# One attention-and-MLP kernel, the same instructions in a newly searched order

## The chip, the cores and the metric

The kernel runs on 1 core of one Trainium2 chip. The metric is the device time of an execution in microseconds (us); lower is better. A core has five engines that run side by side: PE multiplies matrices (PEld is its weight load), DVE and ACT do elementwise work, POOL (GpSimd) does some of that too, and SP issues most of the transfers.

## The reference

Attention over 4 batches, 8 heads, 768 positions and head size 64, in which a position sees itself, the 127 positions before it and the first 4 positions (the "sinks"); then one gated MLP block on the result, with a matrix over the positions.

```python
keep = is_sink | in_window                      # 4 sinks, window 128
a = softmax(where(keep, q @ k.T / 8, -1e9))
x = (a @ v)  as (batch, 768, 512)
h = gelu_tanh(x @ w_in)                         # 512 -> 1024
u, v = h[..., :512], h[..., 512:]
v_n = (v - mean) / sqrt(var + 1e-6) * g_ln
v_s = einsum('ts,bsd->btd', w_sg, v_n) + b_sg   # over the 768 positions
out = x + (u * v_s) @ w_out
```

## The kernel before

The heads are taken two at a time: pair n (0 to 15) holds two heads of batch b = n // 4. All work is cut into 854 named steps. Each step belongs to one engine and is made by a small function; the steps' data dependencies become semaphore waits. What this case is about is the order of the steps. It is written out in two tables: `FIRST` lists all 854 names, and `TAKERS` names the engine for steps that two engines can do. `Planner.run` goes through `FIRST` and emits one step after the other. Every engine then works through its own steps strictly in that order, so a step that waits holds up all later steps of the same engine, and SP's transfers are queued the same way. Buffers are handed out in this order too: a step that needs a buffer waits for the last reader of the tile that had it. There are 4 PSUM banks of the kind called `m` (most matmul results), 2 double banks of the kind called `s` (scores), and 4 buffers each for loaded k, q and v rows and for output rows.

The names, by stage:

- Attention, pair n: `load_k`, `load_q`, `load_v` (SP transfers), `cast_k`, `cast_q`, `cast_v` (to bf16), `turn_k`, `turn_q` (PE transposes into PSUM), `cols_k`, `cols_q` (copies out of PSUM); for pairs 11 to 15 a transposing transfer `dma_k`, `dma_q` on SP takes the place of turn and cols. `sc{n}{g}` are the score matmuls of block group g = 0, 1, 2, `exp{n}{g}` the exponentials on ACT, `band{n}{g}` the masking behind them. For the first four pairs there is no band step: `dark{n}{g}` puts the mask into PSUM ahead of the scores. `pv{n}{c}` multiplies by the values for half c of the positions, and `rcp{n}{c}` and `x{n}{c}` (both DVE) divide by the sums. `turn_x`, `cols_x`, or the transfer `xT`, transpose x.
- Sinks: `raw_a`, `raw_b` load the sinks' values, `low_a` and `low_b` convert them, `vsink_a1` to `vsink_b3` copy them on SP, `zero_*` clear their place. `low_b` stands for 12 pairs, `low_a` for 4. `load_k4` and all later loads stand behind `vsink_b3` on SP.
- MLP, batch b: `hv{b}{j}` and `gelu_v`, `bn` (statistics, DVE), `rstd{b}0` and `rstd{b}3` (POOL, three position tiles each), `shift`, and `vn{b}{j}` (normalised v, DVE or ACT); `hu{b}{f}{m}` and `gelu_u`; `sp{b}{f}{m}a` and `b` (the two halves of the product with w_sg), `gate` and `gT` (DVE); `pj{b}{t}` (product with w_out), `o` (DVE, adds x) and `store`.
- `w_in_v`, `w_in_u`, `wsg0`, `wsg1`, `w_out` load weights on POOL's queue; `turn_w` and `cols_w` transpose w_sg.

The PE order alternates between batches: the attention of batch b + 1 lies between the spatial products of batch b. `exp` and the gelus need different ACT tables, so the gelus of a batch wait until the exponentials of one pair are done.

Of the kernel before, what the change touches and what calls it, by code (L numbers as in the profile page):

```python
# [49 lines left out]
class Planner:  # L50
# [37 lines left out]


FIRST = (  # L90
    "load_k0 iden load_q0 raw_a night blank nil zero_a3 zero_a1 zero_b3 warm zero_a0 dark mask "
# [64 lines left out]
    "peek_DVE copied look"  # L156
)
TAKERS = (
    "zero_a0:ACT zero_a1:DVE zero_a2:DVE zero_a3:DVE low_a:DVE zero_b0:DVE zero_b1:DVE "
    "zero_b2:ACT zero_b3:DVE low_b:POOL cols_g:DVE cols_w0:DVE cols_w1:ACT cols_w2:ACT "  # L160
    "cols_w3:DVE cols_w4:DVE cols_w5:DVE cast_k0:POOL cols_k0:DVE cast_q0:POOL cols_q0:ACT "
    "cols_x0:ACT cast_k1:POOL cols_k1:DVE cast_q1:POOL cols_q1:DVE cols_x1:ACT cast_k2:POOL "
    "cols_k2:DVE cast_q2:DVE cols_q2:DVE cols_x2:DVE cast_k3:POOL cols_k3:ACT cast_q3:POOL "
    "cols_q3:DVE cols_x3:DVE vn00:DVE vn01:DVE vn02:ACT vn03:ACT vn04:DVE vn05:DVE cols_k4:DVE "
    "cols_q4:ACT band41:POOL band42:POOL cols_k5:ACT cols_q5:ACT band51:POOL band52:POOL "
    "cols_k6:ACT cols_q6:ACT band61:POOL band62:POOL cols_k7:ACT cols_q7:ACT band71:POOL "
    "band72:DVE cols_x7:DVE cols_k8:ACT cols_q8:ACT band81:DVE band82:POOL vn10:DVE vn11:DVE "
    "vn12:DVE vn13:DVE vn14:DVE vn15:DVE cols_k9:ACT cols_q9:ACT band91:POOL band92:POOL "
    "cols_k10:ACT cols_q10:ACT band101:POOL band102:POOL band111:POOL band112:POOL cols_x11:ACT "
    "band121:POOL band122:POOL vn20:DVE vn21:DVE vn22:ACT vn23:ACT vn24:ACT vn25:DVE "  # L170
    "band131:POOL band132:POOL band141:POOL band142:POOL band151:POOL band152:POOL cols_x15:ACT "
    "vn30:DVE vn31:ACT vn32:ACT vn33:ACT vn34:DVE vn35:DVE"
)
# [1168 lines left out]
```

## Time and profile before

| what | before |
|---|---|
| time, median of 3 runs | 161.76 us (161.67 to 161.82) |
| the profiled execution's own time | 163.07 us |
| its span, first to last instruction | 161.1 us |
| granted TensorE clock | 0.996 |
| PE busy | 150.1 us, 93% of the span |
| DVE busy | 130.5 us, 81% |
| ACT busy | 107.5 us, 67% |
| POOL busy | 83.6 us, 52% |
| transfers | 32.42 MB, mean 201 GB/s |

The profiled execution took 1.31 us more than the median of the runs. The engines' busy times overlap, so they don't add up to the span. A row of the profile's time line reads: start in us, us taken, engine, line of the kernel, operation, what it writes and reads, how many instructions are merged in it, and in square brackets how long the engine had been idle and what ended that. A row of the table of stretches reads: from and to in us, length, then busy us and number of instructions of PE, PEld, DVE, ACT and POOL, the clock, the share of the transfer engines and GB/s.

### The profile page before, as it was taken

Reading aid. Unit: us, or ns where it says so; the run is one execution under the profiler, and the core shown is the slowest. Engines: PE = TensorE matmul, PEld = TensorE weight load, DVE = VectorE, ACT = ScalarE, POOL = GpSimd, SP = SyncE. Lnnn points to the kernel's source line nnn. Section 1 sums busy time; section 2 is a strip of 40 time slices with the busy share of each in tenths; the row PEclk is TensorE's granted clock in tenths of the full one; section 3 lists DMA queues with packets and bytes.
Section 4 is the critical chain, followed back from the end, with each engine's and each line's share of the span. In section 5 each row is a group of like instructions: output and inputs, shape, how many; then the busy total and the mean of one; then the engine's idle time right before and its main releaser. Section 6 shows DMA issues by size and latency. Waiting matters only on the chain. (4 is left out here: it accounts for less than half of the span.)

```text
span 161.1 us, 4001 instructions
## 1 busy us (share of the span) xinstructions
PE 150.1 (93%) x1547; PEld 87.3 (54%) x1562; DVE 130.5 (81%) x283; ACT 107.5 (67%) x143; POOL 83.6 (52%) x126
## 2 busy tenths in 40 slices
PE   6789999998899999999989999999999999999980
PEld 2335665566656766546556555555556645555540
DVE  7555678695898989969999979868999969888980
ACT  6168878695989877988857778665997168811100
POOL 3465761228688789067975880865579602300000
PEclk9999999999999999999999999999999999999998
DMA  4999999998999986999988889999993340140163
GB/s 146 299 270 305 205 151 206 168 289 231 358 336 240 342 130 163 241 315 234 215 142 209 209 177 216 206 300 257 241 216 114 90 158 0 50 148 4 65 259 141
DMA packets 67877, 32.42 MB, mean 201 GB/s; under 512 B 56564, under 2 KB 64772, under 8 KB 67856
## 3 DMA queue, kind: packets, MB, share of 16 engines
q1 hardware_dynamic: 65328, 29.26, 69.5%
q0 software_dynamic: 2384, 2.75, 10.8%
q8 instruction: 13, 0.21, 0.6%
q10 hardware_dynamic: 144, 0.13, 0.2%
q14 instruction: 8, 0.07, 0.1%
HBM read 24.81 MB, written 6.29 MB: 193 GB/s over the span
## 5 line engine op out<-in xcount | busy, mean ns | idle before, releaser
L627 ACT ACTIVATE ex<-sc 128x1024 bf16<-128x1024 f32 x48 | 47.4, 1024 | 10.5 <-PE sc L610 10.4
L864 PE MATMUL vs<-wsgT,vn 128*128 128x384 bf16 x192 | 35.5, 326 | 1.6 <-DVE vn L840 1.0
L864 PEld LDWEIGHTS <-vn 128*128 128x128 bf16 x192 | 17.5, 98 | 13.2 <-issue 1.6
L793 PE MATMUL hu<-xT,w_in_sb 128*128 128x384 bf16 x128 | 23.4, 326 | 0.0
L801 ACT ACTIVATE uT<-hu 128x384 bf16<-128x384 f32 x32 | 14.9, 490 | 12.3 <-PE hu L793 12.1
L907 PE MATMUL o_ps<-w_out_sb,gT 128*128 128x512 bf16 (+1 forms) x91 | 22.6, 370 | 0.5
L751 PE MATMUL hv<-w_in_sb,xT 128*128 128x512 bf16 x94 | 22.4, 379 | 0.1
L875 DVE SCALAR_TENSOR_TENSOR vs<-vs,g_sb,b_bc 128x384 f32<-128x384 f32 x32 | 19.5, 619 | 2.6 <-PE vs L864 1.3
L773 DVE BATCH_NORM_STATS2 st<-v_all 128x6 f32<-128x512 f32 x24 | 16.3, 678 | 6.5 <-ACT v_all L762 6.5
L311 POOL TENSOR_SCALAR_AFFINE_SELECT ex<-ex 128x512 bf16<-128x512 bf16 (+1 forms) x23 | 15.4, 670 | 9.7 <-ACT ex L627 9.4
L610 PE MATMUL sc<-qT,kT 64*128 64x256 bf16 (+2 forms) x320 | 18.9, 249 | 0.9 <-ACT qT L247 0.5
L249 POOL CAST cast<-k_f 128x768 bf16<-128x768 f32 x16 | 13.4, 840 | 12.0 <-DMA k_f<-in_k_dram 9.4
L676 PEld LDWEIGHTS <-ex 128*128 128x128 bf16 x480 | 16.8, 97 | 4.0 <-issue 1.4
L695 DVE TENSOR_TENSOR x<-av,rcps 128x384 bf16<-128x384 f32 x32 | 17.5, 552 | 0.9
L883 DVE TENSOR_TENSOR gT<-vs,uT 128x384 bf16<-128x384 f32 x32 | 17.5, 555 | 0.9
L676 PE MATMUL av<-v_sb,ex 128*128 128x65 bf16 x352 | 18.0, 194 | 0.1
L249 POOL CAST cast<-q_f 128x768 bf16<-128x768 f32 x15 | 13.0, 869 | 9.7 <-DMA q_f<-in_q_dram 5.0
L918 DVE TENSOR_TENSOR o_sb<-o_ps,x 128x512 f32<-128x512 f32 (+1 forms) x25 | 16.2, 663 | 1.3 <-PE o_ps L907 1.2
L762 ACT ACTIVATE v_all<-hv 128x512 f32<-128x512 f32 x24 | 13.7, 598 | 5.2 <-PE hv L751 5.0
L793 PEld LDWEIGHTS <-w_in_sb 128*128 128x128 bf16 x128 | 12.3, 98 | 8.7 <-issue 0.2
L249 POOL CAST v_sb<-v_f 128x768 bf16<-128x768 f32 x16 | 13.9, 869 | 3.1 <-DMA v_f<-in_v_dram 3.1
L751 PEld LDWEIGHTS <-xT 128*128 128x128 bf16 x96 | 9.2, 98 | 10.5 <-DVE xT L249 0.6
(71 smaller groups left out, 194.2 us busy)
## 6 DMA issues: line engine op xcount, KB each, us to landing
k_f<-in_k_dram SPq DMA_DIRECT2D x16, 384.0 KB, 5.9
q_f<-in_q_dram SPq DMA_DIRECT2D x16, 384.0 KB, 5.2
v_f<-in_v_dram SPq DMA_DIRECT2D x16, 384.0 KB, 6.3
out_dram<-o_sb SPq DMA_DIRECT2D x23, 256.0 KB, 2.2
wsg<-in_moe_w_sg_dram POOLq DMA_DIRECT2D x2, 576.0 KB, 10.8
w_in_sb<-in_moe_w_in_dram POOLq DMA_DIRECT2D x2, 512.0 KB, 8.0
w_out_sb<-in_moe_w_out_dram POOLq DMA_DIRECT2D x1, 512.0 KB, 8.3
b_bc<-in_moe_b_sg_dram SPq DMA_DIRECT2D x1, 384.0 KB
```

Source lines behind the costliest of these rows:

```text
L249: eng[e].tensor_copy(dst, src)
L610: nc.tensor.matmul(sc.tile[row:row + keys, h, col:col + m], kT.tile[rows, k0:k0 + keys], qT.tile[rows, q0:q0 + m], start=not by_pe, stop=n ...
L627: nc.scalar.activation(out=ex.tile, in_=sc.tile, func=AF.Exp, scale=scale)
L676: nc.tensor.matmul(av.tile[:, m, h, :], ex.tile[:, h, col:col + 128], val, start=first, stop=(m == HT - 1 and h == 1 and at == len(steps) ...
L695: nc.vector.tensor_mul(x.tile[:, hp, HT * c:HT * (c + 1), :].rearrange("p i (h d) -> p i h d", h=2), av.tile[:, :, :, 0:64], rcp.to_broadc ...
L751: nc.tensor.matmul(ps.tile[:, 0:512], xT.tile[:, c, 128 * j:128 * (j + 1)], w_in_sb[:, c, DF:], start=(c == 0), stop=(c == KD - 1))
L773: nc.vector.bn_stats(out=st.tile, in_=v_all.tile[:, j, :])
L793: nc.tensor.matmul(ps.tile[:, 0:NH], w_in_sb[:, c, 128 * f:128 * (f + 1)], xT.tile[:, c, NH * m:NH * (m + 1)], start=(c == 0), stop=(c == ...
L864: nc.tensor.matmul(ps.tile[:, 0:NH], vn.tile[:, si, 128 * f:128 * (f + 1)], wsgT[:, si, cols], start=(si == 0), stop=(si == NT - 1))
L875: nc.vector.scalar_tensor_tensor(out=ps.tile[:, 0:NH], in0=ps.tile[:, 0:NH], scalar=g_sb[:, f:f + 1], in1=b_bc[:, cols], op0=ALU.mult, op1 ...
L883: nc.vector.tensor_mul(gT.tile[:, f, cols], ps.tile[:, 0:NH], uT.tile[:, f, cols])
L907: nc.tensor.matmul(ps.tile[:, 0:w], gT.tile[:, c, 128 * t:128 * (t + 1)], w_out_sb[:, c, cols], start=(c == 0), stop=(c == KU - 1))
```

## The change

`FIRST` is replaced by another order of the same 854 names, and `TAKERS` gives 23 steps to another engine. No step is added, removed or altered. Both come from a search that plays the order through on a model of the machine; the new search also played each order through in made-up executions in which transfers land late, all together and by chance, beside the undisturbed one. The 23 steps: from DVE to ACT `zero_a1`, `zero_a2`, `zero_a3`, `cols_q3`, `vn00`, `vn05`, `vn14`, `vn21`, `vn25`; from ACT to DVE `cols_w2`, `cols_k3`, `cols_k10`, `vn03`, `vn22`, `vn24`; from POOL to DVE `low_b`, `cast_k1`, `cast_k3`, `cast_q3`, `band51`, `band61`; from DVE to POOL `low_a`, `band81`.

The lists are long; these are the lines of the diff that hold the places spoken of below.

```diff
 FIRST = (
...
-    "cols_k0 cast_k1 turn_q0 cols_q0 dark00 cast_q1 cast_k2 sc00 dark01 exp00 turn_k1 cols_k1 "
-    "sc01 exp01 vsink_a1 vsink_a2 vsink_a3 load_v0 turn_q1 dark02 sc02 cols_q1 dark10 sc10 exp02 "
-    "turn_k2 load_k3 load_q3 load_v1 exp10 cast_q2 turn_q2 dark11 cols_q2 cast_v0 sc11 dark12 "
...
-    "cols_x3 hv00b gelu_v00 zero_b0 low_b vsink_b1 hold vsink_b2 vsink_b3 hv02 bn00 hv04 hv01a "
...
-    "turn_q4 cols_q4 rstd03 shift03 vn03 vn05 hu030 turn_w5 turn_w3 gelu_u030 vn04 cols_w3 "
...
-    "xT6 cast_v7 load_q9 load_v9 load_k10 load_q10 load_v10 load_k11 pj05 o05 cast_q8 turn_q8 "
...
-    "gelu_u130 hu111 gelu_u101 gelu_u111 hu131 sc90 sc91 shift10 bn14 vn10 vn11 gelu_u131 exp91 "
-    "vn12 load_v11 load_k12 load_q12 rstd13 shift13 vn15 pv80 pv81 vn14 vn13 cast_q10 cast_k11 "
...
-    "x121 sp200b gate200 gT200 sp231a sp231b gate231 band130 gT231 sc131 exp131 sp210a sp210b "
-    "sc132 exp132 sc140 exp140 gate210 gT210 sp211a sp211b gate211 cast_v14 gT211 cast_q15 "
...
+    "cast_k1 low_a zero_a2 vsink_a1 vsink_a2 vsink_a3 dark00 cols_q0 sc00 exp00 dark01 sc01 "
+    "turn_k1 cols_k1 cast_q1 turn_q1 cols_q1 cast_k2 exp01 cast_q2 dark02 turn_k2 sc02 dark10 "
...
+    "cols_x3 hv00a hv00b hv02 wsg1 hv01a hv05 hold gelu_v00 one gelu_v02 low_b vsink_b1 vsink_b2 "
...
+    "cast_q4 turn_k4 turn_q4 cols_q4 cols_k4 hu011 gelu_u011 rstd03 shift03 vn04 vn03 turn_w4 "
+    "cols_w4 turn_w5 sc40 sc41 turn_g cols_g cols_w5 vn05 load_v5 load_k6 load_q6 load_v6 exp40 "
...
+    "exp80 x70 pv71 rcp71 cast_k9 turn_k9 cols_k9 cast_q9 sc81 exp81 sc82 band81 x71 turn_x7 o03 "
+    "cols_x7 o05 pj01 o01 band80 load_v9 cast_v9 hv10 hv11 hv15 exp82 gelu_v10 gelu_v11 bn10 "
...
+    "gelu_v13 turn_q9 cols_q9 hu131 hv14 gelu_v14 hu100 gelu_u100 bn13 bn14 gelu_u131 hu111 "
+    "hu101 gelu_u101 rstd10 shift10 vn10 vn11 vn12 rstd13 hu110 gelu_u110 shift13 vn15 gelu_u111 "
+    "hu120 gelu_u120 vn13 hu121 pv80 gelu_u121 rcp80 vn14 cast_q10 load_k11 load_q11 load_v11 "
+    "load_k12 cast_k11 dma_k11 hu130 x80 load_q12 turn_k10 cols_k10 cast_v10 cast_q11 dma_q11 "
...
+    "dma_q12 sp101a sp101b pv81 rcp81 x81 store05 gate101 xT8 exp100 band100 gT101 sc101 sc102 "
...
+    "cast_q14 band122 o14 vn24 hu231 hu211 hu221 gelu_u221 band120 sp200a sp200b gate200 sc130 "
+    "sc131 gT200 gelu_u211 pv120 rcp120 x120 pv121 rcp121 x121 sp231a sp231b gate231 gelu_u231 "
+    "exp130 band130 exp131 sp211a gT231 cast_v14 cast_k15 load_q15 cast_q15 dma_q14 sp210a "
+    "sp210b gate210 gT210 sp211b gate211 dma_k14 sc132 sc140 gT211 exp132 sp220a sp220b band131 "
...
 )
 TAKERS = (
...
```

More of the change, by code (lines that the diff above doesn't have):

```diff
@@ L90 @@
 FIRST = (
-    "load_k0 iden load_q0 raw_a night blank nil zero_a3 zero_a1 zero_b3 warm zero_a0 dark mask "
[64 rows of a table removed]
-    "peek_DVE copied look"
[65 rows of a table added]
+    "copied look"
 )
 TAKERS = (
-    "zero_a0:ACT zero_a1:DVE zero_a2:DVE zero_a3:DVE low_a:DVE zero_b0:DVE zero_b1:DVE "
-    "zero_b2:ACT zero_b3:DVE low_b:POOL cols_g:DVE cols_w0:DVE cols_w1:ACT cols_w2:ACT "
+    "zero_a0:ACT zero_a1:ACT zero_a2:ACT zero_a3:ACT low_a:POOL zero_b0:DVE zero_b1:DVE "
+    "zero_b2:ACT zero_b3:DVE low_b:DVE cols_g:DVE cols_w0:DVE cols_w1:ACT cols_w2:DVE "
@@ L161 @@
     "cols_w3:DVE cols_w4:DVE cols_w5:DVE cast_k0:POOL cols_k0:DVE cast_q0:POOL cols_q0:ACT "
[L162 to L170, printed above, removed]
+    "cols_x0:ACT cast_k1:DVE cols_k1:DVE cast_q1:POOL cols_q1:DVE cols_x1:ACT cast_k2:POOL "
+    "cols_k2:DVE cast_q2:DVE cols_q2:DVE cols_x2:DVE cast_k3:DVE cols_k3:DVE cast_q3:DVE "
@@ new lines @@
+    "cols_q3:ACT cols_x3:DVE vn00:ACT vn01:DVE vn02:ACT vn03:DVE vn04:DVE vn05:ACT cols_k4:DVE "
+    "cols_q4:ACT band41:POOL band42:POOL cols_k5:ACT cols_q5:ACT band51:DVE band52:POOL "
+    "cols_k6:ACT cols_q6:ACT band61:DVE band62:POOL cols_k7:ACT cols_q7:ACT band71:POOL "
+    "band72:DVE cols_x7:DVE cols_k8:ACT cols_q8:ACT band81:POOL band82:POOL vn10:DVE vn11:DVE "
+    "vn12:DVE vn13:DVE vn14:ACT vn15:DVE cols_k9:ACT cols_q9:ACT band91:POOL band92:POOL "
+    "cols_k10:DVE cols_q10:ACT band101:POOL band102:POOL band111:POOL band112:POOL cols_x11:ACT "
@@ L171 @@
+    "band121:POOL band122:POOL vn20:DVE vn21:ACT vn22:DVE vn23:ACT vn24:DVE vn25:ACT "
     "band131:POOL band132:POOL band141:POOL band142:POOL band151:POOL band152:POOL cols_x15:ACT "
```

103 rows, old and new, of the table FIRST are left out of this document.

## The prediction

> **What bounds the kernel now.** I read the page's busy times first, then the table of stretches cut where the work changes character, then the time line at each place where PE sat idle.
>
> ```profile
> span 161.1 us, 4001 instructions
> PE 150.1 (93%) x1547; PEld 87.3 (54%) x1562; DVE 130.5 (81%) x283; ACT 107.5 (67%) x143; POOL 83.6 (52%) x126
> ```
>
> ```profile
> core 0: us, PE busy (x) PEld busy (x) DVE busy (x) ACT busy (x) POOL busy (x), PEclk, DMA share, GB/s
> 0.00:10.00 10.00, 6.97 (x46) 2.92 (x46) 5.23 (x22) 4.25 (x5) 4.65 (x12) 1.00 0.74 238
> 10.00:26.00 16.00, 15.39 (x259) 9.59 (x260) 11.47 (x25) 13.28 (x15) 8.97 (x12) 1.00 1.11 221
> 26.00:42.00 16.00, 14.91 (x125) 8.96 (x124) 12.12 (x28) 12.05 (x21) 7.27 (x12) 1.00 1.00 238
> 42.00:66.00 24.00, 23.81 (x329) 15.39 (x330) 21.71 (x44) 20.36 (x24) 19.47 (x27) 1.00 0.97 246
> 66.00:82.00 16.00, 14.95 (x132) 8.56 (x130) 13.74 (x28) 13.59 (x21) 10.39 (x15) 1.00 1.08 249
> 82.00:98.00 16.00, 15.89 (x214) 9.66 (x214) 14.79 (x31) 12.17 (x13) 10.50 (x16) 1.00 0.77 191
> 98.00:113.00 15.00, 14.89 (x106) 7.95 (x106) 12.33 (x28) 10.04 (x19) 8.48 (x13) 1.00 1.16 254
> 113.00:130.00 17.00, 16.95 (x211) 10.03 (x212) 16.16 (x35) 11.17 (x12) 11.37 (x19) 1.00 0.63 160
> 130.00:157.00 27.00, 26.33 (x146) 14.19 (x146) 22.84 (x48) 10.62 (x18) 2.51 (x4) 1.00 0.26 98
> ```
>
> PE bounds the kernel. From 10 to 130 us it is idle for 16 - 15.39 + 16 - 14.91 + 24 - 23.81 + 16 - 14.95 + 0.11 + 0.11 + 0.05 = 3.2 us in all. Its work is the same in any order, so an order can win about that, and lose without limit. DVE is second and close: 21.71 of 24 us, 14.79 of 16, 16.16 of 17. Three waits hold most of PE's idle time after the start:
>
> ```profile
> 38.22 0.51 PE L550 MATMUL cps<-iden,cast 128*128 128x128 bf16 x6 [0.47 <-POOL cast L249]
> 41.59 1.62 PE L864 MATMUL vs<-wsgT,vn 128*128 128x384 bf16 x9 [0.57 <-ACT uT L801]
> 81.26 0.66 PE L864 MATMUL vs<-wsgT,vn 128*128 128x384 bf16 x3 [0.99 <-DVE vn L840]
> ```
>
> They are turn_q4, sp000a and sp100b, together 2.0 us. The chain of waits ends in the last store's addition and what follows it (157.19 us), which no step of the change touches.
>
> **The change part by part.** The sum is made against the profiled execution (span 161.1, its own time 163.07 us); the median of the runs is 161.76, 1.31 less, and I carry the difference over unchanged.
>
> *Start to the first w_sg product, 0 to 41.6 us.*
>
> ```profile
> 10.36 0.83 POOL L249 CAST cast<-k_f 128x768 bf16<-128x768 f32 x1 [0.25 <-DMA k_f<-in_k_dram]
> 10.51 0.38 PE L590 MATMUL sc<-ex,iden 128*128 128x512 bf16 x1
> L249 DVE CAST cast<-q_f 128x768 bf16<-128x768 f32 x1 | 0.6, 550 | 0.0
> ```
>
> The loads of k and q set the first 10 us, and their SP order stays. The new PE order puts turn_k2 ahead of sc02. Its cast ends at 10.36 + 0.83 = 11.19, and PE has nothing left after dark02 (about 10.9), so +0.3. The casts of k1, k3 and q3 move from POOL to DVE: 3 x 0.55 = 1.65 us into stretches where DVE is busy 11.47 of 16 us; covered, and at most +0.55 if the last one is not. The +0.3 is gone by 38.22, because there PE waits for the cast of q4 anyway (0.47).
>
> That wait hangs on low_b, which moves from POOL to DVE and stands ahead of the sink copies, behind which load_k4 and load_q4 are issued:
>
> ```profile
> L249 DVE CAST vsink<-raw x1: 949/949/949, 5.7 to 5.7; 4x512 bf16<-4x512 f32 x1
> 27.58 1.46 POOL L249 CAST vsink<-raw 4x1536 bf16<-4x1536 f32 x1
> L840 DVE TENSOR_SCALAR vn<-v_all,mv x16: 514/540/1111, 33.9 to 140.1; 128x512 bf16<-128x512 f32 x16
> ```
>
> DVE never did the 1536-element form. From the 512-element form it would take 3 x 0.95 = 2.85 us, from the cast of q2 2 x 0.55 = 1.1. The first ran beside a POOL cast, and vn shows what that can do (0.54 alone, 1.04 to 1.11 at worst); at 27 us POOL is idle, so I take half of 2.85, 1.4. POOL had to wait for a zero fill on DVE, which is done early now; DVE reaches low_b at about 27.2 and ends at 28.6 against 27.58 + 1.46 = 29.04. I count 0; the ends are -0.7 and +1.1 on the loads of k4 and q4.
>
> ```profile
> 40.35 0.81 ACT L836 ACTIVATE vn<-v_all,mv 128x512 bf16<-128x512 f32 x1 [0.79 <-DVE mv L826]
> 40.17 0.99 DVE L840 TENSOR_SCALAR vn<-v_all,mv 128x512 bf16<-128x512 f32 x2
> ```
>
> The 0.57 at sp000a was for a PSUM bank: gelu_u030, which empties one, stood behind vn03 (40.35 to 41.16) on ACT. The new list has gelu_u011 ahead of vn05 there and leaves a bank free. The last vn still end at 40.17 + 0.99 = 41.16, so sp000a starts near 41.0 and sp000b follows without a gap: -0.5.
>
> *DVE from 42 to 66 us.* band51 and band61 come from POOL; o05 goes behind x71, on which turn_x7 waits.
>
> ```profile
> L636 DVE TENSOR_TENSOR ex<-ex,mask 128x768 bf16<-128x768 bf16 x1 | 0.6, 550 | 0.0
> L918 DVE TENSOR_TENSOR o_sb<-o_ps,x 128x512 f32<-128x512 f32 (+1 forms) x25 | 16.2, 663 | 1.3 <-PE o_ps L907 1.2
> L695 DVE TENSOR_TENSOR x<-av,rcps 128x384 bf16<-128x384 f32 x32 | 17.5, 552 | 0.9
> L249 DVE COPY kT<-cps 128x768 bf16<-128x768 bf16 x4 | 3.8, 950 | 2.7 <-PE cps L550 2.7
> ```
>
> 2 x 0.55 - 0.66 = +0.44 in a stretch where DVE has 2.3 us of slack on paper but is never waited out. I let it through: of the 0.5 gained, 0.1 is left at turn_x7. If there is slack after all, 0.5 stays; if POOL's casts slow the two bands as they slow vn, +0.6 to +1.1 more.
>
> *The wait of 0.99 at sp100b.*
>
> ```profile
> 78.16 3.04 DVE L840 TENSOR_SCALAR vn<-v_all,mv 128x512 bf16<-128x512 f32 x3
> 79.61 0.65 PE L864 MATMUL vs<-wsgT,vn 128*128 128x384 bf16 x3
> 77.40 0.82 POOL L249 CAST cast<-q_f 128x768 bf16<-128x768 f32 x1
> 79.91 1.01 POOL L249 CAST cast<-q_f 128x768 bf16<-128x768 f32 x1
> ```
>
> Three vn take 3.04 us, 1.01 each, while four POOL casts (first and last shown) run back to back. The new order has bn14 ahead of shift10 and rstd13 straight behind rstd10, so the second half starts about 0.5 us sooner, and vn14 is on ACT: two vn of 1.04 are left, and the last ends near 79.9. PE, which began sp100a at 79.61, gets to sp100b at about 79.5, since pv81 (an estimate of 0.56, from its start to sp100a's) now comes later. That is 1.3 gained less 0.56 owed, 0.75 for PE. DVE is less well off: it is relieved of one vn (1.04) but gets cols_k10 (0.95, as the copies of kT above), and still owes rcp81 and x81 (about 0.75, x alone 0.55). From 82 to 98 us it is busy 14.79 of 16, and turn_x11 waits on it (x111). So I pass on only 0.15 of PE's gain there, the part by which DVE itself is ahead: 0.1 + 0.15 = 0.25 us ahead at hv20, bounds 0 and 0.9.
>
> Beside POOL's casts a vn takes 1.04 in place of 0.54. A band moved to DVE may be slowed in the same way, as POOL casts in this stretch for pairs 6 to 8. Two bands at twice 0.55 are +1.1 (rival 4). A rule of the Trainium skill speaks for that, and so against this change: GPSIMD Engine Reference, section 1, Specifications, says that GpSimd's SBUF interfaces are shared with VectorE and contend with DVE instructions that have two SBUF inputs or use both ports. A band has two such inputs; by that rule the sum would be 162.7, by the unslowed row 161.6. The doubled vn agree with it; no row shows which moved band would meet a cast.
>
> *The last attention stretch, 113 to 130 us.*
>
> ```profile
> 98.50 0.81 PE L751 MATMUL hv<-w_in_sb,xT 128*128 128x512 bf16 x2
> 116.53 0.61 PE L610 MATMUL sc<-qT,kT 64*128 64x256 bf16 x8
> 117.07 1.15 PE L864 MATMUL vs<-wsgT,vn 128*128 128x384 bf16 x6
> 116.96 2.85 ACT L627 ACTIVATE ex<-sc 128x1024 bf16<-128x1024 f32 x3 [0.35 <-PE sc L610]
> 120.00 3.99 ACT L627 ACTIVATE ex<-sc 128x1024 bf16<-128x1024 f32 x4 [0.18 <-PE sc L610]
> 124.56 0.63 POOL L311 TENSOR_SCALAR_AFFINE_SELECT ex<-ex 128x512 bf16<-128x512 bf16 x1
> 128.13 0.80 ACT L247 COPY xT<-xps 128x768 bf16<-128x768 bf16 x1 [4.15 <-PE xps L726]
> 129.28 1.03 PE L751 MATMUL hv<-w_in_sb,xT 128*128 128x512 bf16 x4
> ```
>
> The reader is to see the seven exponentials exp132 to exp152 from 116.96 to 123.99, nearly without a gap, 18.5 us behind hv20 (98.50), and the chain from there: band152 (124.56), pv151, x151, turn_x15, cols_x15 (128.13 to 128.93), hv30 (129.28). The new order has sp211a and sp211b ahead of sc132: six matmuls, 1.15 - 0.16 = 1.0 us. All else that stands between hv20 and sc132 is the same; so exp132 to exp152 start about 1.0 us later, counted from hv20. The chain has slack: band152 began 0.57 behind exp152 because POOL still did band151, of which 0.4 goes when the exponentials come later and spread, and hv30 began 0.35 behind cols_x15. So 1.0 - 0.4 - 0.35 = +0.25 is left; the ends are 0 and +1.0.
>
> *Smaller things.* sc130 and sc131 stand together now: 33 separate runs of score matmuls in place of 34. A switch costs PE's weight load this much:
>
> ```profile
> PEld L610 <- issue: 8.8, 32, 0.4
> ```
>
> That is 0.28 a time, half of it given back after the run: -0.15. Stores of batch 2 move back to after 126 us, where the transfers are busy 0.26 of the time: 0. From hv30 to the end the two orders differ in the sequence of equal steps only; shift33 stands behind o20 but vn34 still precedes sp300b: 0.
>
> Sum: -0.25 + 0.25 - 0.15 = -0.15 us, so 163.07 - 0.15 by the profiled execution and 161.6 by the median.
>
> **The rivals.** (1) DVE does not set the pace. Then PE keeps the 0.5 and the 0.75: -1.25 + 0.25 - 0.15 = -1.15, 160.6. For it: PE is fuller than DVE in every stretch, and what DVE does late is seldom waited for. Against: DVE's share in three stretches. (2) The last stretch costs all of its 1.0: -0.25 + 1.0 - 0.15 = +0.6, 162.4. It decides if hv30 again starts 129.28 - 123.99 = 5.3 us behind exp152's end, and not 4.5. For it: every step of that chain is there again. (3) low_b takes 2.85 on DVE: k4 and q4 land 1.1 later, and nothing covers that, since turn_q4 waits already: -0.15 + 1.1, 162.7. The point from which it costs is low_b's end at 29.04. (4) The moved bands are slowed: +1.1 at turn_x7, 162.7; it decides once a moved band takes over 0.8. Against (3) and (4): DVE and POOL are idle enough to miss each other there.
>
> **How the numbers follow.** A measurement of this kernel tells about 0.2% (0.32 us) from no change. The sum's own case has 0.36, with a range of 161.0 to 162.2; of it 0.09 faster, 0.21 within 0.2%, 0.06 slower. Rival 1 has 0.34, rival 2 0.16, rivals 3 and 4 0.07 each. So faster 0.43, same 0.21, slower 0.36. The range runs from rival 1 with half of the 0.7 at the loads (160.6 - 0.35) to rivals 3 and 4 with the 0.25 of the last stretch doubled (162.7 + 0.25): 160.3 to 163.0.
>
> **What would show it.** sp000a without a wait near 41.0; turn_q4 still waiting; turn_x7 at 65.3 to 65.7; sp100b's wait below 0.5; turn_x11 behind x111; exp152 ending about 26.5 us behind hv20 (before 25.5) and hv30 31.0 behind it (before 30.8). The prediction is wrong if PE waits in places that I have not named, most likely for a PSUM bank or a transfer that an SP step ahead of it holds back.

## The result, and the profile after

Before 161.81 us, changed 160.74 us (medians of 20 runs each). The ratio is 0.9927, with a 95 % interval of 0.9905 to 0.995: the changed order is faster by 0.73 %, about 1.2 us (1.07 us by the two medians). The profiled execution of the changed kernel took 161.13 us with a span of 159.4. That of the kernel before took 163.07, 1.3 us above its median, so the difference of the two profiles, 1.7 us of span, is more than what the change is worth. The first two lines of the changed kernel's page:

```profile
span 159.4 us, 4009 instructions
PE 151.4 (95%) x1562; PEld 88.2 (55%) x1562; DVE 134.2 (84%) x284; ACT 108.4 (68%) x146; POOL 80.0 (50%) x121
```

Its stretches with the cuts of the prediction (the columns are length, busy us and instructions of each engine, clock, transfers):

```profile
26.00:42.00 16.00, 15.99 (x136) 9.89 (x137) 12.51 (x30) 13.87 (x23) 7.31 (x11) 1.00 1.10 286
42.00:66.00 24.00, 23.72 (x326) 14.96 (x325) 22.72 (x44) 19.51 (x23) 15.69 (x22) 1.00 0.92 229
66.00:82.00 16.00, 16.00 (x124) 9.23 (x123) 14.19 (x29) 14.30 (x23) 11.95 (x17) 1.00 0.95 214
82.00:98.00 16.00, 15.83 (x225) 9.98 (x224) 14.94 (x33) 11.18 (x13) 9.45 (x15) 1.00 1.07 218
113.00:130.00 17.00, 16.89 (x205) 9.98 (x201) 16.31 (x36) 10.12 (x11) 10.24 (x16) 1.00 0.67 160
```

PE's idle time is gone where it stood before: 1.09 us from 26 to 42 is 0.01 now, 1.05 from 66 to 82 is 0. VectorE is fuller than before in each of these rows (22.72 in place of 21.71 from 42 to 66), and PE's busy time in the three that had little idle time fell by less than 0.1. The time line of PE has no idle time in brackets at any of the three places where it waited:

```profile
37.37 0.83 PE L550 MATMUL cps<-iden,cast 128*128 128x128 bf16 x12
40.43 1.31 PE L864 MATMUL vs<-wsgT,vn 128*128 128x384 bf16 x7
65.25 0.51 PE L726 MATMUL xps<-iden,x 128*128 128x128 bf16 x6
78.64 1.64 PE L864 MATMUL vs<-wsgT,vn 128*128 128x384 bf16 x9
97.22 1.03 PE L751 MATMUL hv<-w_in_sb,xT 128*128 128x512 bf16 x4
128.40 0.81 PE L751 MATMUL hv<-w_in_sb,xT 128*128 128x512 bf16 x3
```

These are turn_k4 with turn_q4 straight behind it, sp000a (41.59 before), turn_x7 (65.67), sp100a, sp100b and sp110a in one run of nine matmuls (before: three, 0.99 idle, three), hv20 (98.50) and hv30 (129.28). The end, as VectorE's last additions show it, first before, then changed:

```profile
155.60 1.35 DVE L918 TENSOR_TENSOR o_sb<-o_ps,x 128x512 f32<-128x512 f32 x3 [0.17 <-PE o_ps L907]
```

```profile
154.72 1.35 DVE L918 TENSOR_TENSOR o_sb<-o_ps,x 128x512 f32<-128x512 f32 x3 [0.18 <-PE o_ps L907]
```

o23y ends at 156.95 and 156.07: 0.9 us earlier. From there to the end of the span it is 4.18 us before and 3.33 now (from the first and last instruction at full precision), so half of the span's 1.7 us lies behind the last addition, in a tail that I had counted at nothing.

The starts of five steps and the end of o23y cut the span into stretches. In them the two profiles differ so (changed less before, us; step times come from counting each engine's instructions in the trace against the written order):

| stretch | predicted | in the two profiles |
|---|---|---|
| start to hv00a | 0 | +0.24 |
| hv00a to sp000a | -0.5 | -1.40 |
| sp000a to turn_x7 | +0.4 | +0.74 |
| turn_x7 to hv20 | -0.15 | -0.87 |
| hv20 to hv30 | +0.25 - 0.15 | +0.40 |
| hv30 to o23y | 0 | 0.00 |
| tail | 0 | -0.85 |
| sum | -0.15 | -1.74 |

### The profile page after: what moved, and what is told of

Its sections match the earlier page's. It is cut to its first block, busy times and chain, and to the rows that moved or that the text cites. A ratio compares the mean times of both kernels' runs of the same rounds, so it can differ in the third digit from the quotient of the medians.

```text
span 159.4 us, 4009 instructions
## 1 busy us (share of the span) xinstructions
PE 151.4 (95%) x1562; PEld 88.2 (55%) x1562; DVE 134.2 (84%) x284; ACT 108.4 (68%) x146; POOL 80.0 (50%) x121
## 3 DMA queue, kind: packets, MB, share of 16 engines
HBM read 24.81 MB, written 6.29 MB: 195 GB/s over the span
## 4 chain that ended last, share of the span: by engine, by line
PE 63%; DVE 16%; DMA 9%; POOL 4%; issue 3%; SPq 2%; ACT 0%; POOLq 0%; DVEq 0%
PE vs L864 14%; PE o_ps L907 10%; PE hv L751 10%; DMA k_f<-in_k_dram 8%; PE av L676 7%; PE hu L793 7%; PE sc L610 7%; DVE x L695 3%; PE cps L550 3%; PE sc L590 3%; DVE ex L638 2%; DVE vs L875 2%; DVE gT L883 2%; POOL mv L820 2%; DVE vn L840 2%
## 5 line engine op out<-in xcount | busy, mean ns | idle before, releaser
L864 PEld LDWEIGHTS <-vn 128*128 128x128 bf16 x192 | 17.3, 98 | 11.8 <-issue 1.1
L907 PE MATMUL o_ps<-w_out_sb,gT 128*128 128x512 bf16 (+1 forms) x100 | 23.3, 371 | 0.2 <-DVE x L695 0.2
L801 ACT ACTIVATE uT<-hu 128x384 bf16<-128x384 f32 x32 | 14.8, 491 | 11.9 <-PE hu L793 11.6
L311 POOL TENSOR_SCALAR_AFFINE_SELECT ex<-ex 128x512 bf16<-128x512 bf16 (+1 forms) x22 | 14.6, 666 | 16.2 <-ACT ex L627 15.5
L751 PE MATMUL hv<-w_in_sb,xT 128*128 128x512 bf16 x96 | 21.9, 379 | 0.0
L249 POOL CAST v_sb<-v_f 128x768 bf16<-128x768 f32 x16 | 13.3, 840 | 6.6 <-DMA v_f<-in_v_dram 6.6
L249 POOL CAST cast<-k_f 128x768 bf16<-128x768 f32 x14 | 12.0, 856 | 7.3 <-DMA k_f<-in_k_dram 5.6
```

What stands on the lines that cost most here:

```text
L249: eng[e].tensor_copy(dst, src)
L751: nc.tensor.matmul(ps.tile[:, 0:512], xT.tile[:, c, 128 * j:128 * (j + 1)], w_in_sb[:, c, DF:], start=(c == 0), stop=(c == KD - 1))
L864: nc.tensor.matmul(ps.tile[:, 0:NH], vn.tile[:, si, 128 * f:128 * (f + 1)], wsgT[:, si, cols], start=(si == 0), stop=(si == NT - 1))
L907: nc.tensor.matmul(ps.tile[:, 0:w], gT.tile[:, c, 128 * t:128 * (t + 1)], w_out_sb[:, c, cols], start=(c == 0), stop=(c == KU - 1))
```

## The experiments

Theory A: PE sets the pace, and what it gains in one stretch stays. Theory B, the prediction's: VectorE sets the pace from 42 to 98 us and takes most of a gain back. The kernels e1 to e3 and e11 are made of the two lists: up to a named step the one order, from there what is left in the other, each step on the engine that its list gives it. e0 and e5 to e9 ran once, for their profile; a ratio with its 95 % interval is given for the others.

**e0: the kernel before, profiled again.**

> The kernel before, once more, for its profile alone: how far do two profiles of one and the same order agree? If the step times repeat, TensorE reaches sp000a at 41.59, turn_x7 at 65.67, hv20 at 98.50, hv30 at 129.28 and ends o23y at 156.95 us again, each within 0.1, and differences of 0.3 us between two orders can be read from one profile each. If they scatter by 0.3 or more, they can't. The tail from o23y's end to the end of the span (4.15 us here, 3.30 in the changed kernel) should come out between the two if it is chance.

```profile
39.49 0.49 PE L864 MATMUL vs<-wsgT,vn 128*128 128x384 bf16 x2 [0.40 <-ACT uT L801]
96.78 0.59 PE L751 MATMUL hv<-w_in_sb,xT 128*128 128x512 bf16 x2
```

sp000a comes at 39.49, not 41.59: the same order is 2.1 us earlier in another execution. The head does not repeat. The loads are the likely reason: load_q1 landed at 9.22 in the first profile and at 7.82 here, and turn_q4 did not wait. Behind the head times do repeat: hv20 to hv30 30.78 in both, hv30 to o23y 27.67 in all fourteen profiles of this study. From sp000a to turn_x7 it takes 24.08 and 24.39, from there to hv20 32.84 and 32.90. So from hv20 on one profile each is enough; ahead of it, and in the head above all, several are needed.

The first 25 us scatter most: hv00a starts between 24.61 and 27.52 us over the fourteen profiles. Against e0 the changed kernel's span is not shorter but 0.36 longer (159.40 against 159.04), because its profile reaches hv00a 1.51 later; from hv00a to the end it is 1.15 ahead of e0 and 1.97 ahead of the first profile. Seven profiles with before's order up to hv00a (three of them with the small changes of e4, e10 and e11) have it at 25.7 in the mean, seven with the changed one at 26.0: what the new order does there is not shown.

**e1: the changed head alone, e2: the changed middle alone, e3: both.**

```
e1: after-list up to sp000a | before-list
e2: before-list up to hv10 | after-list up to hv20 | before-list
e3: after-list up to sp000a | before-list up to hv10 | after-list up to hv20 | before-list
```

> The changed list up to sp000a, then the rest in the order and with the engines of before. Theory A (TensorE alone sets the pace, a gain of the head is kept by whatever comes behind it): sp000a near 40.4 as in the changed kernel (before 41.6), and the 1.1 us still there at turn_x7, hv20, hv30 and the end: about 160.6 us, ratio 0.993. Theory B (the prediction's: VectorE sets the pace from 42 to 66 and gives a gain back): at most 0.4 us left at turn_x7 although the order there is that of before, the ratio within 0.997 to 1.0.

> The list of before up to hv10, the changed one from hv10 to hv20, before's again behind it. Theory A: sp100b's wait is gone and TensorE is 0.9 us ahead at hv20 (97.6 in place of 98.5) and still at hv30 and at the end: ratio 0.9945. Theory B: VectorE, 92 % busy from 82 to 98 us, lets only 0.15 to 0.25 us through to hv20: ratio 0.9985 to 1.0.

> The changed list up to sp000a and from hv10 to hv20, the order of before from sp000a to hv10 and from hv20 on: the two stretches in which the changed kernel's profile is ahead, without the two in which it falls back (0.75 us from sp000a to turn_x7, 0.4 from hv20 to hv30). Theory A: 1.15 + 0.87 = 2.0 us ahead of before, ratio 0.9875, which beats the changed kernel by 1.1 us. Theory B: no better than the changed kernel, 0.993, since VectorE takes back what TensorE gains.

Ratios: e1 0.9936 (0.9907 to 0.9966), e2 0.9942 (0.9909 to 0.9976), e3 0.9885 (0.9831 to 0.9939). 0.64 % and 0.58 % add up to 1.22 %; e3 has 1.15 %. PE at sp000a, turn_x7 and hv20 in e1, then at turn_x7, sp100a and hv20 in e2, and at hv20 and hv30 in e3:

```profile
39.90 0.66 PE L864 MATMUL vs<-wsgT,vn 128*128 128x384 bf16 x3
64.00 0.51 PE L726 MATMUL xps<-iden,x 128*128 128x128 bf16 x6
96.96 0.81 PE L751 MATMUL hv<-w_in_sb,xT 128*128 128x512 bf16 x3
```

```profile
64.57 0.51 PE L726 MATMUL xps<-iden,x 128*128 128x128 bf16 x6
77.96 1.31 PE L864 MATMUL vs<-wsgT,vn 128*128 128x384 bf16 x7
96.55 1.03 PE L751 MATMUL hv<-w_in_sb,xT 128*128 128x512 bf16 x4
```

```profile
95.50 0.81 PE L751 MATMUL hv<-w_in_sb,xT 128*128 128x512 bf16 x3
126.32 1.03 PE L751 MATMUL hv<-w_in_sb,xT 128*128 128x512 bf16 x4
```

e1 needs 64.00 - 39.90 = 24.10 us for the stretch that took 24.08 in the first profile of before: VectorE, reached 1.7 us sooner, took nothing back. e2 needs 96.55 - 64.57 = 31.98 from turn_x7 to hv20, before 32.84 and 32.90: 0.9 gained and kept. hv20 to hv30 is 126.32 - 95.50 = 30.82 in e3, as before. Theory B falls: in none of the three does VectorE's load take a gain back. That the gains of stretches add fits the ratios, but these are wide (e3's interval is 0.6 to 1.7 %), and e1's ratio holds a gain of the tail too, 3.34 us there against 4.03 in e2 and 3.81 to 4.18 before (see e10). e3 (159.82 us, median of 6) is the fastest kernel of those that were timed in several runs; its interval lies below 1, and overlaps that of the changed kernel.

One row of e3 goes beyond both theories: from turn_x7 to hv20 it takes 31.59, and e2 31.98 with the same order and engines there. The difference lies at pj11, which is 0.38 us earlier in e3. In e2, POOL's mask step ahead of VectorE's band, the band, and PE at pj11:

```profile
86.16 0.64 POOL L311 TENSOR_SCALAR_AFFINE_SELECT ex<-ex 128x512 bf16<-128x512 bf16 x1 [0.79 <-ACT ex L627]
86.33 1.01 DVE L638 TENSOR_TENSOR ex<-ex,mask 128x1024 bf16<-128x1024 bf16 x1
88.56 1.04 PE L907 MATMUL o_ps<-w_out_sb,gT 128*128 128x512 bf16 x4 [0.17 <-DVE x L695]
```

In e3, band and mask step:

```profile
85.15 0.68 DVE L638 TENSOR_TENSOR ex<-ex,mask 128x1024 bf16<-128x1024 bf16 x1
85.50 0.83 POOL L311 TENSOR_SCALAR_AFFINE_SELECT ex<-ex 128x512 bf16<-128x512 bf16 x1 [0.94 <-ACT ex L627]
```

Where POOL starts 0.17 us ahead, the band takes 1.01 in place of 0.68; the band 4.4 us ahead of it does the same (1.03 in e2, 0.68 in e3). VectorE then comes late to the division x on which pj11 waits. The changed kernel has the two long bands as well (1.03 and 1.00).

**e4: low_b alone.**

```
 TAKERS  low_b:POOL -> low_b:DVE
 FIRST   zero_b0 from behind gelu_v00 to behind dark30
```

> The order of before; low_b alone goes to VectorE, and the fill zero_b0 that it needs moves ahead to dark30, where VectorE has room. Three profiles of before's order take 15.71, 14.88 and 15.23 us from hv00a to sp000a, the three with the changed head 14.31, 14.31 and 14.32. Theory L (the loads of k4 and q4 come too late, by chance more or less, and the sink copies behind low_b hold them): load_k4 is issued about 3.8 us behind hv00a in place of 5.2, turn_q4 waits for nothing, and 14.85 us are left (the bank's wait at sp000a stays, 0.64 against an unhindered step): a gain of 0 to 0.9 by the execution, some 0.4 in the mean, ratio about 0.9975. Theory R (the rest of the new order made it): turn_q4 waits as before, 15.2 in the mean, ratio 1.0.

The cast low_b and the first load behind it in the changed kernel (load_k4 was issued at 31.08 before):

```profile
26.89 0.94 DVE L249 CAST vsink<-raw 4x1536 bf16<-4x1536 f32 x1
```

```profile
29.82 0.40 SPq L455 DMA_DIRECT2D k_f<-in_k_dram  x1
```

and in e4, where hv00a started at 27.52 in a late execution:

```profile
28.22 0.94 DVE L249 CAST vsink<-raw 4x1536 bf16<-4x1536 f32 x1
```

```profile
31.21 0.40 SPq L455 DMA_DIRECT2D k_f<-in_k_dram  x1
```

```profile
38.76 0.83 PE L550 MATMUL cps<-iden,cast 128*128 128x128 bf16 x12
42.12 1.06 PE L864 MATMUL vs<-wsgT,vn 128*128 128x384 bf16 x5 [0.22 <-ACT uT L801]
```

The load goes out 3.7 us behind hv00a in place of 5.2, turn_q4 runs straight behind turn_k4, and hv00a to sp000a takes 14.6. Theory L holds in the one profile. Five profiles with before's order there gave 14.8 to 15.7 (mean 15.1), seven with the changed one 14.31 to 14.32 (e11, whose seam at hv00a costs 1.1, apart): the wait for q4 was a matter of chance (0.47 us, 0.10, and none in three), and the new order is out of its reach. It is the smaller part: hv00a to turn_q4 is 11.8 us in the mean of the five and 11.58 in the changed kernel, turn_q4 to sp000a, where the wait for the bank lay, 3.3 and 2.73.

On the order of before a part of an early head is lost again behind sp000a (e0, e4, e10: 24.39, 24.61 and 24.86 us from sp000a to turn_x7 in place of 24.08). In e0 and e10 turn_k5 is 0.2 and 0.6 us late behind POOL's cast of k5; in e0 that cast waits for its load, in e10 the profile does not settle what it waits for. In e4 that cast is done, and VectorE is late: its last two vn take 2.08 us beside POOL's casts of k5 and q5, in place of 0.54 each,

```profile
40.71 2.08 DVE L840 TENSOR_SCALAR vn<-v_all,mv 128x512 bf16<-128x512 f32 x2
```

so that sp000b waits for them, sp010a comes 0.2 late, and sp030a waits 0.16 for VectorE's gT. The ratio is 0.9908 (0.9879 to 0.9937), more than the 0.9975 I expected and no worse than the whole change's 0.9927; the intervals overlap, so the ratios don't rank the two. The tail (3.66 us here) makes up a part of the gain, the rest I can't place.

**e5: band51 back on POOL.**

```
 TAKERS  band51:DVE -> band51:POOL     (on the changed kernel)
```

> The changed kernel with band51 back on POOL, all else as it is. From sp000a to turn_x7 TensorE does the same steps in 24.08 us before and 24.82 changed. Theory S (VectorE's late and slow band51, 52.86 to 54.03, holds pv50): pv50 waits for nothing and 24.4 to 24.5 us are left; what remains over 24.1 is the new sequence of matmuls. Theory V (VectorE's whole load sets the pace there): 24.1 or less. Theory W (the sequence of matmuls alone): still 24.8.

24.32 us from sp000a to turn_x7, and pv50 waits for nothing: theory S as to that execution. But e6, e8 and e9, which leave this stretch as the changed kernel has it, took 24.36, 24.32 and 24.81. What differs is who comes first. In the changed kernel's profile, VectorE's band51, POOL's cast of k8 and PE at pv50:

```profile
52.86 1.17 DVE L636 TENSOR_TENSOR ex<-ex,mask 128x768 bf16<-128x768 bf16 x1
```

```profile
52.79 0.82 POOL L249 CAST cast<-k_f 128x768 bf16<-128x768 f32 x1
```

```profile
54.08 0.23 PE L676 MATMUL av<-v_sb,ex 128*128 128x65 bf16 x2 [0.21 <-DVE ex L636]
```

In e6 the same two instructions:

```profile
52.19 0.55 DVE L636 TENSOR_TENSOR ex<-ex,mask 128x768 bf16<-128x768 bf16 x1
```

```profile
52.31 1.11 POOL L249 CAST cast<-k_f 128x768 bf16<-128x768 f32 x1
```

The cast 0.07 us ahead: the band takes 1.17 in place of 0.55. The band 0.12 ahead: it takes 0.55, and the cast 1.11 in place of 0.82. e9 repeats the first (cast 53.95, band 54.02 for 1.16), e8 has them apart by 0.7. It costs PE 0.46 to 0.5 us at turn_x7, by chance, in two of four executions. So e5 alone can't show theory S, as e6 and e8 gained the same without its edit; the two outcomes of one and the same order do. Theory V gave 24.1 or less and fails.

**e6: sp211a and sp211b behind sc132 and sc140 again.**

```
-sp211a ... sp210a sp210b ... sp211b gate211 dma_k14 sc132 sc140
+... sp210a sp210b ... dma_k14 sc132 sc140 sp211a sp211b gate211
```

> The changed kernel with sp211a, sp211b and gate211 put behind sc132 and sc140, as they stood before. hv20 to the end of exp152 is 26.62 us in the changed kernel and 25.49 before, hv20 to hv30 31.18 and 30.78. The prediction's step (the six matmuls ahead of sc132 push the exponentials by 1.0, of which slack behind exp152 gives back about 0.7): exp152 ends 25.6 to 25.8 behind hv20 and hv30 comes 30.8 behind it. Rival (TensorE is full there, and its sequence of matmuls costs the 0.4): exp152 goes back by 1.0 and hv30 stays at 31.2.

ACT's exponentials exp132 to exp152 in the changed kernel, then in e6:

```profile
116.47 1.94 ACT L627 ACTIVATE ex<-sc 128x1024 bf16<-128x1024 f32 x2 [1.57 <-PE sc L610]
118.62 3.96 ACT L627 ACTIVATE ex<-sc 128x1024 bf16<-128x1024 f32 x4 [0.21 <-PE sc L610]
122.82 1.02 ACT L627 ACTIVATE ex<-sc 128x1024 bf16<-128x1024 f32 x1 [0.23 <-PE sc L610]
```

```profile
114.28 1.94 ACT L627 ACTIVATE ex<-sc 128x1024 bf16<-128x1024 f32 x2 [0.45 <-PE sc L610]
117.41 3.96 ACT L627 ACTIVATE ex<-sc 128x1024 bf16<-128x1024 f32 x4 [1.19 <-PE sc L610]
121.61 1.02 ACT L627 ACTIVATE ex<-sc 128x1024 bf16<-128x1024 f32 x1 [0.23 <-DVE rcps L689]
```

exp132 goes back by 1.1 us (18.1 behind hv20 at 96.16, in place of 19.25), the wait moves behind exp140, and exp152 still ends 26.47 behind hv20; hv30 comes at 31.03. e5, with the changed order here, has 26.45 and 31.01. So the place of sp211 is worth nothing: neither theory of this run holds.

**e8 and e9: what else stands ahead of sc152.** I had compared the two lists only up to sc132. Up to sc152 they differ in sp230a, sp230b and sp201a.

```
e8: sp230a sp230b gate230 gT230 sp201a moved to behind sc152   (on the changed kernel)
e9: the same, and turn_x15 ahead of sp221b
```

> The changed kernel with sp230a, sp230b and sp201a put behind sc152, as they stood before (they are the only steps between hv20 and sc152 that the two orders do not share). hv20 to the end of exp152 is 25.49 us in six profiles of before's last stretch, 26.45 to 26.62 in three of the changed one; hv20 to hv30 is 30.78 and 31.01 to 31.18. Theory C (the chain from exp152 to hv30 carries the loss): exp152 ends 25.2 to 25.5 behind hv20 and hv30 comes at 30.8. Theory P (TensorE's own sequence carries it: sp221b stands ahead of turn_x15, so only pj21 is left to cover cols_x15): exp152 goes back by a microsecond and hv30 stays at 31.0.

> As e8, and turn_x15 put ahead of sp221b, as it stood before. Theory C: no different from e8. Theory P: with x151 early and sp221b over the copy cols_x15, hv30 comes 30.7 to 30.85 behind hv20.

hv20 to hv30 is 31.83 in e8 and 32.59 in e9, worse than anything. PE's waits in e8 have a new line:

```profile
PE sc L610 <- ACT ex L627: 0.7, 2, 0.5
```

The three steps were what PE did while ACT worked on an exponential and no score bank was free. Both theories miss: with the fillers gone sc150 and sc151 wait 0.7, and exp152 gains only half a microsecond. From these runs the last stretch is a balance of scores, fillers and exponentials, 0.23 us slower in the new order (31.01 against 30.78), and which step carries that 0.23 stays open.

**e7: vn14 and cols_k10 on their old engines.**

```
 TAKERS  vn14:ACT -> vn14:DVE   cols_k10:DVE -> cols_k10:ACT   (on e2)
```

> The kernel e2 (changed list from hv10 to hv20 alone) with vn14 back on VectorE and cols_k10 back on ACT. e2 takes 31.98 us from turn_x7 to hv20, before 32.83 to 32.90. If the engine of vn14 made the gain: three vn of 1.04 stand in a row again, sp100b waits 1.0 to 1.2 us and hv20 comes 32.8 to 33.1 behind turn_x7. If the new order made it (rstd13 straight behind rstd10, pv81 later): sp100b waits 0.5 at most and hv20 comes within 32.4. If VectorE's load decides at hv20, the 0.95 that cols_k10 takes off it gives most of that back: 32.0.

```profile
78.75 1.12 PE L864 MATMUL vs<-wsgT,vn 128*128 128x384 bf16 x5 [0.24 <-DVE vn L840]
```

The third vn stands on VectorE again, and PE waits 0.24 inside sp100b and is 0.54 behind e2 at sp110a; at hv20 it is 0.16 behind (32.14 against 31.98), because the wait ahead of pj11 is gone. That cols_k10 off VectorE took it away is not shown: in e3, with cols_k10 on VectorE, it is gone too, and in both the bands take 0.68. So 0.7 of the 0.86 comes from the order (bn14 ahead, rstd13 at once, pv81 later); the engines' share is 0.16 against e2 and 0.55 against e3.

**e10: three more instructions on VectorE.**

```
-put("one", ... nc.vector.tensor_copy(one, iden[:, 0:KU]) ...
+put("one", ... the same copy, four times ...
```

> The kernel before with the copy 'one' (0.16 us, VectorE, near 20 us) done four times over, so VectorE has three instructions more and nothing else differs. In ten profiles the last transfer of the instruction queue q14 ahead of the end starts at a fixed place in VectorE's list that moves with the number of its instructions: +0.3 us from o23y's end with 331, -0.3 and -0.6 with 333, -1.4 with 334 and 335, -2.15 with 336; and the tail from o23y's end to the end of the span goes along: 4.03, 4.18 and 3.81, 3.4 to 3.7, 3.3. Theory F (that transfer is VectorE's instructions and delays the last stores): the tail falls to about 3.3 us, 0.5 to 0.9 less, ratio about 0.996. Theory N (chance, or the order in the head): 3.8 to 4.2 as before, ratio 1.0.

```profile
span 159.8 us, 4004 instructions
```

```profile
16.80 2.60 DVE L429 CAST one<-iden 128x4 f32<-128x4 bf16 x4
155.09 1.35 DVE L918 TENSOR_TENSOR o_sb<-o_ps,x 128x512 f32<-128x512 f32 x3 [0.17 <-PE o_ps L907]
```

```profile
20.32 0.40 PE L610 MATMUL sc<-qT,kT 64*128 64x256 bf16 x4 [0.80 <-DVE qT L249]
```

o23y ends at 156.45, and the tail is 3.31 us, on the order of before: theory F, and the transfer starts 2.15 us ahead of o23y's end as in the changed kernel. The ratio shows no gain, 0.9984 (0.9947 to 1.002): the four copies took 2.60 us, not 0.64, and held sc30 up by 0.80. (The one copy of before took 0.50 us at 17.63; 0.16 is the changed kernel's.) The first and the third copy took the time, 1.38 and 0.78 us; both end within 0.02 us of a cast on POOL that ran beside them:

```profile
16.80 1.38 DVE L429 CAST one<-iden 128x4 f32<-128x4 bf16 x1
17.31 0.85 POOL L249 CAST v_sb<-v_f 128x768 bf16<-128x768 f32 x1
```

**e11: a version put together from the best parts.**

```
before-list up to hv00a | after-list up to sp000a | before-list up to hv10
| after-list up to hv20 | before-list; sc130 moved down to sc131; "one" five times
```

The expectation says four copies more, which are these five in all.

> The order of before up to hv00a, the changed one to sp000a, before's to hv10, the changed one to hv20, before's to the end, with sc130 moved down to sc131 (one switch to score matmuls less) and four copies of 'one' more on VectorE. If the stretches add: 0.2 at hv00a against e3, 14.31 us to sp000a, 24.1 to turn_x7, 31.6 to 32.0 to hv20, 30.5 to hv30 (30.8 without the merged score matmuls), a tail of 3.3: about 159.2 us, ratio 0.984 to 0.987. If gains are given back behind the seams: 0.9885 as e3 or worse.

0.9957 (0.9926 to 0.9989): e3's median is better by 0.7 %, though the intervals overlap. The profile shows where time goes: sc30 waits 0.6 for VectorE behind the copies, hv00b 1.1 for cols_x3, which the seam at hv00a put behind a zero fill on VectorE, and hv20 to hv30 takes 31.01 in place of 30.78, though one switch to score matmuls is saved: with sc130 gone from there, hu231 waits 0.21 for a bank that VectorE's o empties, and pv120 starts no sooner than before (13.38 us behind hv20, before 13.40). The tail is 3.29 as expected.

## Why the prediction was right or wrong

The time (160.74) is in the range, and 0.9 below the figure of 161.6. Rival 1 gave 160.6. The range was wide enough for a sum whose main step failed, and that rival 1 comes so close is in part luck, since terms that it lacks, on both sides, nearly cancel.

*The step that failed: "I let it through" and "I pass on only 0.15".* VectorE's busy share was taken for a pace. e1 and e2 show that PE keeps what it gains: 24.10 us against 24.08 behind an earlier start, and 0.9 us kept at hv20. The mechanism at sp100b was right (wait gone, 0.75 forecast for PE, 0.87 to 0.9 measured at hv20, 1.25 in e3). What VectorE took back, some 0.4 ahead of pj11, less than the 0.6 that I put down, was not its load: with the same load e3 has no wait there. It came from two bands that POOL's mask steps stretched, which is rival 4's mechanism at bands that I had not named. turn_x11 starts 0.24 behind x111's end, as forecast.

*The loads of k4 and q4.* I counted 0, bounds -0.7 and +1.1. low_b took 0.94 on VectorE, below my lower bound of 1.1, and load_k4 left 1.26 us earlier. The forecast that turn_q4 still waits was wrong. In the two profiles the stretch gained 1.40; against the mean of five profiles with before's order, 0.8, of which 0.2 lies at turn_q4. I had read one profile's 0.47 as a constant.

*sp000a.* Right: no wait, 40.43. The 0.5 forecast here is 0.6 in the mean of the five, the larger part of the 0.8.

*42 to 66 us.* +0.4 forecast, +0.74 in the profile, +0.24 to 0.28 in executions without the collision (24.32 and 24.36 against 24.08). The reason was another: a new sequence of matmuls (argued, not tested alone), and rival 4's mechanism, which did come: band51 took 1.17, over the 0.8 at which I said it decides, at 0.5 us for one band and in half of the executions. The Trainium skill (GPSIMD Engine Reference, section 1, Specifications) says that GpSimd's SBUF interfaces contend with VectorE instructions that have two SBUF inputs; these rows agree, as the band has two, and whichever of it and POOL's cast starts second runs longer (1.17 in place of 0.55, 1.11 in place of 0.82).

*The last stretch.* exp152 26.6 behind hv20 (forecast 26.5), hv30 4.56 behind it (4.5) and 31.18 behind hv20 (31.0); 31.01 in e5. The sizes were right and the cause was not: sp211a and sp211b move exp132, not exp152 (e6). The row of score switches did fall,

```profile
PEld L610 <- issue: 7.5, 28, 0.4
```

from 32 to 28, but in e11 merging sc130 with sc131 gains nothing.

*The tail.* Counted at 0, -0.85 in the profiles. No rival had it; e10 shows that it follows the number of VectorE's instructions.

So rival 1's figure came about, its reason holds (PE sets the pace), but its sum is not the measured one: the loads and the tail gave more, the stretch from 42 to 66 took more. Over the profiles' means the stretches behind hv00a add up to some -1.7 us (head -0.8, 42 to 66 +0.3, to hv20 -0.9, last stretch +0.3 to +0.4, tail -0.7), more than the 1.2 of the runs; a part may be lost ahead of hv00a, and the rest stays open.

## What to carry to other kernels

A busy engine beside a busier one is no pace: before letting it take a gain back, look for a place where the bounding engine waits for it. Where one and the same step takes two different times, see what the other engine had started just before it. Profile the unchanged kernel twice before reading a wait behind a load as a constant; what sits there by chance is what a robust order removes. When a step is late, compare everything ahead of it in both orders, and take a filler away only when you know what it fills.

## What the runs showed of the hardware that I had not expected

*A late transfer of instructions, and a tail that follows it.* The trace has a queue of instruction transfers. From 156.6 to 157.0 us in before, around o23y's end, and from 153.8 to 154.3 in the changed kernel, two microseconds ahead of it, that queue moved one packet (queue, packets, MB, share):

```profile
q14 instruction: 1, 0.01, 4.8%
```

```profile
q14 instruction: 1, 0.01, 3.9%
```

Counted over all of VectorE's instructions in the trace, waits included: with 331 this transfer starts 0.3 us behind o23y's end and the tail is 4.03 us (two profiles), with 333 0.3 to 0.6 ahead and 3.8 to 4.2 (two), with 334 and 335 1.4 ahead and 3.4 to 3.7 (three), with 336 and 337 2.15 ahead and 3.28 to 3.34 (seven). e10 changed only that number in the kernel and got the short tail. That the transfer carries VectorE's own instructions is inferred from its place, which follows their number. Whether it delays the last stores' packets, or VectorE's own way to the end, isn't settled.

*Two engines' instructions 0.1 us apart have two outcomes.* The band and the cast above: the one that starts first runs at or near its own time, the other takes 0.3 to 0.6 us longer. The fourteen traces hold 196 mask multiplies on VectorE. In 93 of them a cast or mask step of POOL had started earlier and still had 0.15 us or more to run: they took longer by what it had left, less 0.12 to 0.14 us, at most by 0.62. The other 103 took 0.55 us (128x768) or 0.68 (128x1024), within 0.02.

*A tiny copy can be caught too.* The 128x4 copy took 0.16 us where POOL was idle and 1.38 where it ended with POOL's cast, though it has little to move; in e10 the two copies between casts took 0.17 each.
